# An S4 convolution beside a gated linear unit: the second factor of the kernel K built from 33 angles instead of by doublings, on one core

## The chip, the core and the metric

The kernel runs on one core of a Trainium2 chip. The engines named below are TensorE (PE, with PEld for its weight loads), VectorE (DVE), ScalarE (ACT), GpSimd (POOL) and SyncE (SP), whose queue issues all of this kernel's transfers. Each engine runs its own instructions in order and waits on semaphores for the others. The metric is the time of one execution on the device in microseconds, the median over runs; single executions vary by about one per cent.

## What is computed

From `x` (2048 positions, 512 channels) the reference mixes two results, `g` being one sigmoid for each position:

```python
g = sigmoid((x * gate_w).sum(-1))
# a: diagonal state space model, 128 complex states for each channel
logdA = dt * A;  dB = dt * Bc                      # dt = exp(log_dt)
K = einsum("dn,dnl,dn->dl", Cc, exp(logdA[:, :, None] * l), dB).real   # l = 0 .. 2047
y = irfft(rfft(pad(u)) * rfft(pad(K))) + u * Dskip # long convolution of length 2048
# b: gated linear unit
h = sigmoid(x @ w_gate) * (x @ w_up)               # 512 -> 1792
b = h @ w_down                                     # 1792 -> 512
out = g * a + (1 - g) * b
```

Everything is fp32. The part that matters here is `K`: for each of 512 channels and 2048 positions a sum over 128 states of a coefficient times a power of a complex number.

## The kernel before

The work has two threads. One is the convolution: `rows` (16 blocks of `x`: the gate's sums, a first transform, written to DRAM), `kgen` (the kernel `K`, 16 groups of 32 channels, its first transform, written to DRAM), `finish` (16 steps over frequencies: second transforms of `u` and `K`, their product, an inverse transform) and `final` (16 blocks: last transform, mixing, output). The other is `glu`, a generator which issues the gated linear unit in pieces. `UNITS` = 2016 counts its matmuls of 512 columns: 1344 in `hidden` (L401, three for each product, since every fp32 operand is split in a high and a low part) and 672 in the down projection (L339). `run_b(n)` draws pieces until n more units are dealt out.

The program deals these units out between the steps of the convolution: 24 at first, `ROW` = 32 after every fourth block of `rows`, `MID` = 50 for every half group of `kgen`, then 0.7 of what is left over the 16 steps of `finish`, and the rest in `final`. The order in the program gives the instructions their priority; a scheduler of the framework then puts each engine's instructions into a fixed order, so pieces of `glu` and `kgen` are mixed on every engine.

`kgen` has the 128 states in the partitions and for each channel d needs K at 2048 = 32 x 64 positions. A position is split in two numbers, and the power into two factors; `kps` (L220) sums over the states with one matmul for each channel and for the real and the imaginary part, [32 x 64] at a time. Before, both factors are built by doublings on DVE. `bases(pp, gi)` (L147) loads the group's parameters and gives `bz`, the 11 powers z^(2^k) of the step exp(dt A): 704 angles and exponents (L162), rounded (L163, L164), one Exp, Abs and two Sin of 352 elements on ACT (L165 to L168), and the product (L171). `double` (L180) extends a row of powers to twice its length by a complex product: three DVE instructions, L187 to L189. The tile `T` holds three parts: the first factor with the coefficient, and the two halves of the second factor. Four of the doublings (L207 to L209) extend both factors at once, the last of them 2048 elements for each instruction; a sixth one (L213), also 2048, makes the second half of the second factor. `bz` has two buffers, `T` one. Between the two `yield`s stand `bases` of the next group and the last doubling; behind it, at high priority, `kps`, its copy `kst` on ACT (L223), `Dskip` added on DVE (L225), 32 matmuls with `wk` (L232) and four copies `kev` on ACT (L236).

In `hidden` ACT makes `sg`, the sigmoid of a gate block (L408), DVE the product `h` (L409), ACT its high part `hh` (L410), DVE the low part `hl` (L411). `weights` splits weights in the same way (L381, L382 on ACT; L384, L385 on DVE in the first half). `rows` has two more sigmoids for each block (L361, L362). A change between Exp, Sin and Sigmoid on ACT shows in the trace as an ACT_TABLE_LOAD.

Of the kernel before, what the change touches and what calls it, by code (L numbers as in the profile page):

```python
# [28 lines left out]
P = 128  # L30
# [5 lines left out]
KS = [6, 0, 7, 1, 8, 2, 9, 3, 10, 4, 5]  # L36
NB = len(KS)
# [6 lines left out]
ROW, MID, END, LAST = 32, 50, 0.7, 0.14  # L44


def constants():
# [18 lines left out]
    for k in range(32):  # L66
# [7 lines left out]
    e2 = 2.0 ** np.array(KS)  # L74
# [3 lines left out]
        "c_pw": f(np.stack([e2, e2 / (2 * np.pi) * np.where(np.array(KS) < 6, -1, 1)]), 1, 2 * NB),  # L78
# [4 lines left out]
def body(ctx, tc, xp, xt, prm, ldt, dsk, gw, wgu, wdn, c_wu, c_wf, c_wk, c_w2, c_wv, c_pw, out):  # L83
# [22 lines left out]
    pw = cst.tile([P, 2, NB], F32, name="pw")  # L106
# [37 lines left out]
    def tmp(pp):  # L144
        return pp.tile([P, 2048], F32, tag="tmp", bufs=2, name="tmp")

    def bases(pp, gi):  # L147

        pg = pp.tile([P, 6, 32], F32, name="pg")
# [5 lines left out]
        nc.vector.tensor_tensor(aa, pg[:, 0:2], dg, op=OP.mult)  # L155
        sh = [P, 2, NB, 32]
        t = tmp(pp)
        m = NB * 32
        th, sc = (t[:, 2 * m * a:2 * m * (a + 1)].rearrange("p (c k b) -> p c k b", c=2, k=NB) for a in range(2))
        af = t[:, 4 * m:5 * m].rearrange("p (k b) -> p k b", k=NB)  # L160
        n = af.bitcast(I32)
        nc.vector.tensor_tensor(th, aa[:, :, None, :].to_broadcast(sh), pw[:, :, :, None].to_broadcast(sh), op=OP.mult)  # L162
        nc.scalar.activation(n, th[:, 1], AF.Copy)  # L163
        nc.vector.tensor_tensor(th[:, 1], th[:, 1], n, op=OP.subtract)  # L164
        nc.scalar.activation(th[:, 0], th[:, 0], AF.Exp)  # L165
        nc.scalar.activation(af, th[:, 1], AF.Abs)
        nc.scalar.activation(sc[:, 1], th[:, 1], AF.Sin, scale=2 * math.pi)
        nc.scalar.activation(sc[:, 0], af, AF.Sin, scale=-2 * math.pi, bias=hpi)  # L168

        bz = pp.tile([P, 3, NB, 32], F32, name="bz", bufs=2)  # L170
        nc.vector.tensor_tensor(bz[:, 0:2], sc, th[:, 0:1].to_broadcast(sh), op=OP.mult)  # L171
        nc.scalar.activation(bz[:, 2], bz[:, 1], AF.Copy, scale=-1.0)
        w = pp.tile([P, 3, 2, 32], F32, name="w")
        cb = lambda c: pg[:, 4 + c:5 + c].to_broadcast([P, 2, 32])
        nc.vector.tensor_tensor(w[:, 2], pg[:, 2:4], dg, op=OP.mult)
        nc.vector.tensor_tensor(w[:, 0], w[:, 2], cb(0), op=OP.mult)
        nc.vector.tensor_tensor(w[:, 1], w[:, 2], cb(1), op=OP.mult)
        return bz, w

    def double(pp, dst, src, bz, k, nd, e):  # L180
# [324 lines left out]
```

## Time and profile before

| what | value |
|---|---|
| median of three runs | 755.97 us (750.52 to 758.19) |
| the profiled execution, its own time | 753.36 us |
| its span in the trace | 751.6 us |
| busy PE, DVE, ACT | 706.8, 604.9, 375.5 us |
| granted TensorE clock, mean | 0.975 |
| bytes moved | 118.64 MB, mean 158 GB/s |

The three stages follow each other in time: `rows` and the first groups to some 104 us, `kgen` to some 565 us, then `finish` and `final`; `glu` runs beside all of them. A row of a busy time merges overlapping instructions; a mean duration is that of one instruction. A matmul of 512 columns lasts 402 ns in the trace, but the next one starts before it ends, so distances between starts tell more of TensorE than durations. In a row of groups the part behind the second bar is the idle time of the engine just before these instructions and what ended most of it.

### The profile page before, as it was taken

The numbers are of one execution on the slowest core, as the hardware profiler recorded it, in microseconds if no ns is written. First come the engines' busy times: TensorE is split into PE (matmuls) and PEld (weight loads), VectorE is DVE, ScalarE is ACT, GpSimd is POOL, SyncE is SP. The second block draws the span as 40 slices with busy tenths as digits, with TensorE's granted clock in tenths as the row PEclk, the third lists the DMA queues.
The fourth block names the chain that finished last, engine by engine and source line by source line (L and its number), as shares of the span: only waits on it lengthen the run. The fifth ranks groups of instructions, "written<-read, shape, count | busy, mean of one in ns | idle before, by whom it ended". The sixth has DMA issues, their size and how long they took to land.

```text
span 751.6 us, 12658 instructions
## 1 busy us (share of the span) xinstructions
PE 706.8 (94%) x5024; PEld 475.2 (63%) x5024; DVE 604.9 (80%) x835; ACT 375.5 (50%) x611; POOL 3.7 (0%) x36
## 2 busy tenths in 40 slices
PE   4988889998999999999999999999999999999995
PEld 3445348877888778877787787887883323333651
DVE  5888989999999999899999898999944544454343
ACT  5364645763638274655565654546134555555200
POOL 0000000000000000000000000000000000000000
PEclk9789879999999999999999999999999999999999
DMA  6768662433025033565013350531158877774587
GB/s 221 213 204 229 170 178 97 156 104 148 32 88 183 22 115 130 194 237 175 26 57 126 100 189 8 168 115 56 57 187 284 258 241 243 225 223 147 174 285 254
DMA packets 61019, 118.64 MB, mean 158 GB/s; under 512 B 8224, under 2 KB 22944, under 8 KB 59936
## 3 DMA queue, kind: packets, MB, share of 16 engines
q1 hardware_dynamic: 60960, 117.84, 48.3%
q8 instruction: 39, 0.64, 0.3%
q14 instruction: 20, 0.16, 0.1%
HBM read 75.35 MB, written 42.47 MB: 157 GB/s over the span
## 4 chain that ended last, share of the span: by engine, by line
PE 53%; DVE 28%; ACT 8%; DMA 7%; issue 3%; SPq 0%; DVEq 0%; ACTq 0%
PE gups L401 19%; PE dps L339 12%; PE fps L248 9%; DVE T L189 6%; DVE T L188 6%; DVE tmp L187 6%; PE ips L281 4%; PE fps L367 3%; DVE h L409 2%; PE kps L220 2%; DVE hl L411 2%; DMA xs<-xt 2%; PE fps L232 2%; DMA wst<-wgu 1%; PE fps L293 1%
## 5 line engine op out<-in xcount | busy, mean ns | idle before, releaser
L401 PE MATMUL gups<-xh,gu 128*128 128x512 f32 x896 | 293.9, 402 | 15.2 <-ACT gu L381 12.5
L401 PEld LDWEIGHTS gups<-xh,gu 128*128 128x128 f32 x896 | 170.0, 191 | 71.4 <-issue 16.2
L401 PE MATMUL gups<-xl,gu 128*128 128x512 f32 x448 | 179.2, 400 | 0.0
L339 PE MATMUL dps<-dnw,hh 128*128 128x512 f32 x448 | 150.2, 402 | 3.6 <-ACT hh L410 3.0
L187 DVE TENSOR_TENSOR tmp<-T,bz 128x64 f32<-128x64 f32 (+2 forms) x96 | 114.8, 1195 | 2.3 <-issue 0.2
L189 DVE TENSOR_TENSOR T<-T,tmp 128x64 f32<-128x64 f32 (+2 forms) x96 | 114.6, 1194 | 0.7
L188 DVE TENSOR_TENSOR T<-T,bz 128x64 f32<-128x64 f32 (+2 forms) x96 | 114.6, 1193 | 0.0
L339 PEld LDWEIGHTS dps<-dnw,hh 128*128 128x128 f32 x448 | 83.5, 189 | 37.5 <-issue 11.6
L401 PEld LDWEIGHTS gups<-xl,gu 128*128 128x128 f32 x448 | 85.6, 191 | 27.4 <-issue 10.3
L339 PE MATMUL dps<-dnw,hl 128*128 128x512 f32 x224 | 89.6, 401 | 3.0 <-DVE hl L411 1.7
L408 ACT ACTIVATE sg<-gups 128x512 f32<-128x512 f32 x56 | 33.5, 598 | 70.3 <-PE gups L401 69.6
L268 DVE TENSOR_TENSOR t<-fps,uf 128x512 f32<-128x512 f32 x32 | 22.0, 688 | 57.6 <-PE fps L248 47.6
L410 ACT ACTIVATE hh<-h 128x512 fp32r<-128x512 f32 x56 | 35.1, 628 | 47.9 <-DVE h L409 47.9
L409 DVE TENSOR_TENSOR h<-gups,sg 128x512 f32<-128x512 f32 x56 | 38.1, 684 | 20.4 <-PE gups L401 20.1
L339 PEld LDWEIGHTS dps<-dnw,hl 128*128 128x128 f32 x224 | 42.3, 189 | 16.5 <-DVE hl L411 3.7
L411 DVE TENSOR_TENSOR hl<-h,hh 128x512 fp32r<-128x512 f32 x56 | 38.3, 686 | 8.9 <-ACT hh L410 8.4
L381 ACT ACTIVATE gu<-wst 128x1024 fp32r<-128x1024 f32 x28 | 29.6, 1057 | 29.4 <-PE gups L401 13.8
L345 DVE SCALAR_TENSOR_TENSOR acc<-dps,omg,acc 128x512 f32<-128x512 f32 x48 | 35.5, 746 | 10.3 <-PE dps L339 10.3
L248 PE MATMUL fps<-au,w_in 128*64 128x512 f32 x128 | 42.3, 611 | 0.3 <-DVE t L268 0.3
L236 ACT ACTIVATE kev<-fps 128x256 f32<-128x256 f32 x64 | 33.8, 678 | 16.3 <-PE fps L232 15.4
L248 PE MATMUL fps<-ak,w_in 128*64 128x512 f32 x128 | 41.2, 609 | 0.0
L367 PE MATMUL fps<-u,wu 64*128 64x512 f32 x64 | 32.4, 780 | 6.6 <-DMA u<-xp 2.9
(78 smaller groups left out, 664.5 us busy)
## 6 DMA issues: line engine op xcount, KB each, us to landing
wst<-wgu SPq DMA_DIRECT2D x28, 512.0 KB, 4.5
a_u<-evu SPq DMA_DIRECT2D x32, 256.0 KB, 3.3
a_k<-kev SPq DMA_DIRECT2D x8, 1024.0 KB, 6.0
au<-a_u SPq DMA_DIRECT2D x16, 512.0 KB, 4.8
ak<-a_k SPq DMA_DIRECT2D x16, 512.0 KB, 4.2
b_s<-evb SPq DMA_DIRECT2D x32, 256.0 KB, 2.5
b_in<-b_s SPq DMA_DIRECT2D x16, 512.0 KB, 4.6
wsd<-wdn SPq DMA_DIRECT2D x28, 256.0 KB, 3.5
```

What stands on the lines that cost most here:

```text
L187: nc.vector.tensor_tensor(t2, src, sb, op=OP.mult)
L188: nc.vector.tensor_tensor(dst, src, br, op=OP.mult)
L189: nc.vector.tensor_tensor(dst, dst, t2[:, :, ::-1], op=OP.add)
L236: nc.scalar.activation(kv[i][:, s:s + 4], p4[:, :, :, 16 * i:16 * i + 16], AF.Copy)
L248: mm(p[64 * kb:64 * kb + 64], w[:, kb, 64 * c:64 * c + 64], a(kb), start=True, stop=True, tile_position=(0, 64 * kb), skip_group_check=True)
L339: mm(p, a[:, hs], dnw[:, b], start=(n == 0), stop=(n == last))
L345: nc.vector.scalar_tensor_tensor(accs[t], p, omg[:, t:t + 1], accs[t], op0=OP.mult, op1=OP.add)
L367: mm(ph[jp], wu[r, jp], u[r], start=True, stop=True, tile_position=(64 * jp, 0))
L401: mm(p, gu[:, a, k, dc], b[:, dc], start=(n == 0), stop=(n == 11))
L409: nc.vector.tensor_tensor(h, pp[1], sg, op=OP.mult)
L410: nc.scalar.activation(hh, h, AF.Copy)
L411: nc.vector.tensor_tensor(hl, h, hh.bitcast(F32), op=OP.subtract)
```

## The change

The second factor is no longer built by doublings. Its entry q, for q = 0 to 63, is the magnitude exp(q Re) times the cosine and sine of q - 32 angles; the rotation by 32 angles that this leaves out goes into the first factor's coefficient. Since the cosine of -k is that of k and the sine its negative, 33 angles (0 to 32) serve for all 64 entries. `bases` now computes for each of 32 channels 38 angles (these 33, and 64, 128, 256, 512 and 1024 for the doublings of the first factor): 1216 elements for each of product, rounding, subtraction, Abs and two Sin. Before it, the angle of one step is divided by 2 pi and rounded by itself (`tn`). The five exponentials for the doublings are one Exp of 160 elements; the 64 magnitudes of each channel are one Exp of 64 elements with that channel's exponent as a pointer scale, 32 instructions for each group, into `mg`. `B`, the second factor, is three DVE products: cosines and sines for q of 32 and more (2048 elements), and cosines, then negated sines for q under 32, read backwards (1024 each). The first factor keeps five doublings, now alone (`T` without the other halves: 64, 128, 256, 512, 1024 elements), and its coefficient is made and multiplied by that rotation in six small instructions. `ex`, `mg`, `bz` and `B` have one buffer each. `MID` goes from 50 to 45. The constants `c_pw` grow from 22 to 107 numbers. The program's scratch space for software-made DMA descriptors is set to 1024 bytes, which leaves more SBUF; the memsets on POOL and the copy L204 go.

```diff
-KS = [6, 0, 7, 1, 8, 2, 9, 3, 10, 4, 5]
-NB = len(KS)
+ANGLES = list(range(33)) + [64 << k for k in range(5)]
+NA = len(ANGLES)
...
-ROW, MID, END, LAST = 32, 50, 0.7, 0.14
+ROW, MID, END, LAST = 32, 45, 0.7, 0.14
...
     def bases(pp, gi):
...
+        tn = pp.tile([P, 32], I32, name="tn")
+        e5 = pp.tile([P, 5, 32], F32, name="e5")
+        ex = pp.tile([P, 32, 2, NA], F32, name="ex")
+        mg = pp.tile([P, 32, 64], F32, name="mg")
+        f, cs = ex[:, :, 1], ex[:, :, 0]
+        af = mg.rearrange("p d q -> p (d q)")[:, :32 * NA].rearrange("p (d a) -> p d a", d=32)
         n = af.bitcast(I32)
...
+        V.tensor_scalar(aa[:, 1], aa[:, 1], 1 / (2 * math.pi), None, op0=OP.mult)
+        A.activation(tn, aa[:, 1], AF.Copy)
+        V.tensor_tensor(aa[:, 1], aa[:, 1], tn, op=OP.subtract)
+        V.tensor_tensor(f, aa[:, 1, :, None].to_broadcast([P, 32, NA]), pw[:, None, :NA].to_broadcast([P, 32, NA]), op=OP.mult)
+        sh = [P, 5, 32]
+        V.tensor_tensor(e5, aa[:, 0:1].to_broadcast(sh), pw[:, NA:NA + 5, None].to_broadcast(sh), op=OP.mult)
+        A.activation(n, f, AF.Copy)
+        V.tensor_tensor(f, f, n, op=OP.subtract)
+        A.activation(af, f, AF.Abs)
+        A.activation(cs, af, AF.Sin, scale=-2 * math.pi, bias=hpi)
+        A.activation(f, f, AF.Sin, scale=-2 * math.pi)
+        A.activation(e5, e5, AF.Exp)
+        for d in range(32):
+            A.activation(mg[:, d], pw[:, NA + 5:], AF.Exp, scale=aa[:, 0, d:d + 1])
+        bz = pp.tile([P, 3, 5, 32], F32, name="bz")
+        trig = ex[:, :, :, 33:].rearrange("p d c k -> p c k d")
+        V.tensor_tensor(bz[:, 0::2], trig, e5[:, None].to_broadcast([P, 2, 5, 32]), op=OP.mult)
+        A.activation(bz[:, 1], bz[:, 2], AF.Copy, scale=-1.0)
...
     def kgen(pp):
...
-            for k in range(1, 5):
-                e = 2 ** k
-                double(pp, T2[:, :, :, e:2 * e], T2[:, :, :, 0:e], bz, 2 * k, 64, e)
+            T = pp.tile([P, 32, 2, 32], F32, name="T")
+            B = pp.tile([P, 32, 2, 64], F32, name="B")
+            V.tensor_tensor(w[:, 2, 0], w[:, 0, 0], w[:, 1, 1], op=OP.subtract)
+            V.tensor_tensor(w[:, 2, 1], w[:, 0, 1], w[:, 1, 0], op=OP.add)
+            V.tensor_tensor(w[:, 0], w[:, 2], ex[:, None, :, 0, 32].to_broadcast([P, 2, 32]), op=OP.mult)
+            V.tensor_tensor(w[:, 1], w[:, 2], ex[:, None, :, 1, 32].to_broadcast([P, 2, 32]), op=OP.mult)
+            V.tensor_tensor(T[:, :, 0, 0], w[:, 0, 0], w[:, 1, 1], op=OP.add)
+            V.tensor_tensor(T[:, :, 1, 0], w[:, 0, 1], w[:, 1, 0], op=OP.subtract)
+            V.tensor_tensor(B[:, :, :, 32:], ex[:, :, :, :32], mg[:, :, None, 32:].to_broadcast([P, 32, 2, 32]), op=OP.mult)
+            lo = ex[:, :, :, 32:0:-1]
+            V.tensor_tensor(B[:, :, 0, :32], mg[:, :, :32], lo[:, :, 0], op=OP.mult)
+            V.scalar_tensor_tensor(B[:, :, 1, :32], mg[:, :, :32], -1.0, lo[:, :, 1], op0=OP.mult, op1=OP.mult)
+            for k in range(4):
+                double(pp, T[:, :, :, 1 << k:2 << k], T[:, :, :, 0:1 << k], bz[:, :, k], 32, 1 << k)
             yield 1
             if gi + 1 < NG:
                 nxt = bases(pp, gi + 1)
-            double(pp, T[:, 2], T[:, 1], bz, 10, 32, 32)
+            double(pp, T[:, :, :, 16:], T[:, :, :, :16], bz[:, :, 4], 32, 16)
...
-                        mm(p[32 * j:32 * j + 32, s].rearrange("p (a b) -> p a b", a=2), T[:, 0, ch, c], T[:, 1:3, ch, c],
+                        mm(p[32 * j:32 * j + 32, s], T[:, ch, c], B[:, ch, c],
...
-    nc.sync.dma_start(pw, c_pw.to_broadcast([P, 2 * NB]).rearrange("p (a b) -> p a b", a=2))
+    nc.sync.dma_start(pw, c_pw.to_broadcast([P, NA + 69]))
...
-    nc = bacc.Bacc("TRN2", target_bir_lowering=False, num_devices=1)
+    nc = bacc.Bacc("TRN2", target_bir_lowering=False, num_devices=1, dynamic_dma_scratch_size=1024)
```

More of the change, by code (lines that the diff above doesn't have):

```diff
@@ L163, in bases @@
[L163 to L171, printed above, removed]
@@ L172, in bases @@
-        nc.scalar.activation(bz[:, 2], bz[:, 1], AF.Copy, scale=-1.0)
+        tn = pp.tile([P, 32], I32, name="tn")
[4 more added lines that the diff above has]
+        af = mg.rearrange("p d q -> p (d q)")[:, :32 * NA].rearrange("p (d a) -> p d a", d=32)
+        n = af.bitcast(I32)
+        V.tensor_tensor(aa, pg[:, 0:2], dg, op=OP.mult)
+        V.tensor_scalar(aa[:, 1], aa[:, 1], 1 / (2 * math.pi), None, op0=OP.mult)
```

39 lines of the change are left out of this document (11 added, 28 removed).

## The prediction

> **What bounds the kernel now.** I read the page first (busy times, then the chain that ended last), then cut the span into three stages with the windows view, at the ACT copies of the second and the sixteenth group's `kps` (L223, at 103.73 and 548.15 us), and then took prices of single instructions.
>
> ```profile
> PE 706.8 (94%) x5024; PEld 475.2 (63%) x5024; DVE 604.9 (80%) x835; ACT 375.5 (50%) x611; POOL 3.7 (0%) x36
> ...
> PE 53%; DVE 28%; ACT 8%; DMA 7%; issue 3%; SPq 0%; DVEq 0%; ACTq 0%
> PE gups L401 19%; PE dps L339 12%; PE fps L248 9%; DVE T L189 6%; DVE T L188 6%; DVE tmp L187 6%; PE ips L281 4%; PE fps L367 3%; DVE h L409 2%; PE kps L220 2%; DVE hl L411 2%; DMA xs<-xt 2%; PE fps L232 2%; DMA wst<-wgu 1%; PE fps L293 1%
> ```
>
> TensorE is busy 94% and half of the chain, but DVE holds 28% of the chain, most of it the doublings L187 to L189. The windows tell where (columns: stretch, length, busy us and instructions of PE, PEld, DVE, ACT, POOL, then granted clock, DMA share, GB/s):
>
> ```profile
> 0.00:103.73 103.73, 80.59 (x462) 44.99 (x462) 85.95 (x153) 51.04 (x101) 0.63 (x8) 0.84 0.70 205
> 103.73:548.15 444.42, 432.25 (x3879) 348.87 (x3880) 428.08 (x543) 244.63 (x377) 3.03 (x28) 1.00 0.34 114
> 548.15:751.60 203.45, 193.91 (x686) 81.31 (x686) 90.84 (x140) 79.85 (x133) 0.00 (x0) 0.99 0.70 230
> ```
>
> Stage A (rows and the first two groups) is 103.7 us, stage B (14 groups of `kgen`) 444.4, stage C (`finish`, `final`) 203.5. In B, DVE is busy 428.1 of 444.4 (96%), 30.6 us per group; ACT only 244.6 (55%), 17.5 per group. A group takes 31.7 us.
>
> PE's busy time overstates it, since matmuls overlap. What PE must issue is worked out from runs without a gap: 18 GLU matmuls in 4.08 us, 0.227 us for each unit; and a group's 128 `kps` and 32 `wk` matmuls take 1.97 (`wk`, L232) and 1.99 us (`kps`, L220). The chain by time (start, length) and the timeline have the rows:
>
> ```profile
> 412.56 4.08 PE dps L339 x18
> ...
> 736.07 4.04 DMA out<-o
> 742.12 4.59 DMA b_in<-b_s
> ```
>
> ```profile
> 402.64 1.97 PE L232 MATMUL fps<-wk,kst 128*64 128x128 f32 x32
> ...
> 427.26 1.99 PE L220 MATMUL kps<-T 128*32 128x64 f32 x128
> ```
>
> The GLU matmuls that ran in B (windows by line: L401, then L339; the count stands behind PE's busy time):
>
> ```profile
> 103.73:548.15 444.42, 257.75 (x1087) 202.25 (x1088) 1.00 0.34 114
> ...
> 103.73:548.15 444.42, 128.27 (x516) 94.66 (x516) 1.00 0.34 114
> ```
>
> 1603 units in 14 groups are 114.5 a group: 26.0 us, and with `kps` and `wk` 30.0 of 31.7. So in B, DVE is full and PE waits for it only 1.8 us per group, 25 us in all. This is what a lighter DVE can win there; the rest of PE's work is the same before and after. In C, PE is busy 193.9 of 203.5, and nothing of the change is in C but the units moved there.
>
> **The change, part by part.** DVE's prices:
>
> ```profile
> L187 DVE TENSOR_TENSOR tmp<-T,bz 128x2048 f32<-128x2048 f32 x32 | 73.1, 2285 | 0.2
> ...
> L187 DVE TENSOR_TENSOR tmp<-T,bz 128x1024 f32<-128x1024 f32 x16 | 19.5, 1221 | 0.3
> ...
> L171 DVE TENSOR_TENSOR bz<-tmp 128x704 f32<-128x704 f32 x16 | 14.2, 885 | 0.1
> L162 DVE TENSOR_TENSOR tmp<-aa,pw 128x704 f32<-128x704 f32 x16 | 14.1, 883 | 0.0
> ...
> L187 DVE TENSOR_TENSOR tmp<-T,bz 128x64 f32<-128x64 f32 x16 | 4.3, 269 | 1.1
> ...
> L177 DVE TENSOR_TENSOR w<-w,pg 128x64 f32<-128x64 f32 x16 | 3.5, 219 | 0.0
> ```
>
> From 1024 and 2048 elements a product costs 0.157 us and 1.04 ns per element. Removed per group: doublings 3 x (0.27 + 0.42 + 0.69 + 1.22 + 2 x 2.29) = 21.5; the bases' three large products 0.88 + 0.89 + 0.52, four of 0.22 and two of 0.21: 3.6. Together 25.1. Added: two products of 32 x 38 = 1216 elements, 1.42 each; two of 160 and 320, 0.32 and 0.49; twelve small ones of `aa`, `w` and `T` at 0.21, 2.5; `B` from 2048 elements and twice 1024, 2.29 + 2 x 1.22 = 4.7; five doublings of one factor alone 3 x (0.27 + 0.29 + 0.42 + 0.69 + 1.22) = 8.7. Together 19.5. DVE saves 5.6 us per group, 30.6 to 25.0. `B` reads 32 angles backwards, which no row shows; the nearest rows, 1024 and 2048 elements, bound such an op at 1.22 and 2.29, so at worst 2 us of the 5.6 are lost, and DVE is still under PE. I take 1.22.
>
> ACT's prices and table loads:
>
> ```profile
> L381 ACT ACTIVATE gu<-wst 128x1024 fp32r<-128x1024 f32 x28 | 29.6, 1057 | 29.4 <-PE gups L401 13.8 <-DMA wst<-wgu 13.5 <-issue 2.0
> L408 ACT ACT_TABLE_LOAD x22 | 28.2, 1283 | 0.7 <-PE gups L401 0.4
> L167 ACT ACT_TABLE_LOAD x16 | 20.5, 1283 | 0.3
> L165 ACT ACT_TABLE_LOAD x15 | 19.2, 1283 | 0.2
> ...
> L343 ACT ACTIVATE acc<-dps,omg 128x512 f32<-128x512 f32 x16 | 10.8, 684 | 15.8 <-PE dps L339 15.6
> ...
> L368 ACT ACTIVATE evu<-fps 128x512 f32<-128x512 f32 x16 | 9.5, 591 | 15.0 <-PE fps L367 14.2 <-DMA a_u<-evu 0.6
> L168 ACT ACTIVATE tmp<-tmp,hpi 128x352 f32<-128x352 f32 x16 | 9.2, 577 | 0.0
> L167 ACT ACTIVATE tmp<-tmp 128x352 f32<-128x352 f32 x16 | 8.0, 499 | 0.2
> ...
> L204 ACT ACTIVATE T<-bz 128x64 f32<-128x64 f32 x16 | 5.0, 315 | 0.0
> ```
>
> 352 and 1024 elements give 0.21 us and 0.83 ns per element, and a pointer operand adds 0.08 to 0.09 (L168 against L167, L343 against L368). Back to back, each starts 0.09 us before the one ahead ends:
>
> ```profile
> 73.64 0.20 ACT L361 ACTIVATE g<-gl 128x1 f32<-128x1 f32 x1
> 73.73 0.19 ACT L362 ACTIVATE omg<-gl 128x1 f32<-128x1 f32 x1
> 73.82 0.19 ACT L361 ACTIVATE g<-gl 128x1 f32<-128x1 f32 x1
> ```
>
> Removed per group: six of 352 elements and L204, 7 instructions, 3.4 us less 7 x 0.09 = 2.7. Added: three of 1216 elements at 1.22 and one with a pointer at 1.30, `tn`, `e5` and the negated copy 0.24 + 2 x 0.34, and 32 exponentials of 64 elements with a pointer scale. The last are shown by no row: below by the one-element sigmoids (0.09 from start to start), above by L204's 0.315 plus the pointer's 0.09 less the overlap, 0.31. I take the line, 0.207 + 0.053 + 0.082 - 0.09 = 0.25, nearest to L204 in size but without its scattered output: 8.0 us. Added in all 3 x 1.13 + 1.21 + 0.65 + 8.0 = 13.2, net 10.5 us per group (5.4 to 12.4 between the ends).
>
> Then the table loads. Each change of function set costs 1.28 us, and a sigmoid that falls between two sines brings two:
>
> ```profile
> 163.97 1.28 ACT L167 ACT_TABLE_LOAD   x1
> 165.26 0.50 ACT L167 ACTIVATE tmp<-tmp 128x352 f32<-128x352 f32 x1
> 165.78 1.28 ACT L408 ACT_TABLE_LOAD   x1
> 167.07 0.60 ACT L408 ACTIVATE sg<-gups 128x512 f32<-128x512 f32 x1
> 167.56 0.62 ACT L382 ACTIVATE dnw<-wsd 128x512 fp32r<-128x512 f32 x1
> 168.21 1.28 ACT L168 ACT_TABLE_LOAD   x1
> 169.50 0.59 ACT L168 ACTIVATE tmp<-tmp,hpi 128x352 f32<-128x352 f32 x1
> ```
>
> Loads before are 22 + 16 + 15 and a few more, 3.7 per group, three of them unavoidable. In B 1087 / 24 = 45 sigmoids `sg` fall (24 matmuls for each), 3.2 a group. The exponentials take some 8 us of ACT alone, 10 to 11 with what is put between; 1.0 `sg` should fall among them, two loads, in place of 0.1 now: I take 1.8 extra loads, 2.3 us, with 0 and 4 (5.1 us) as ends. Fewer GLU units per group (below) take off 10 x 0.08 = 0.8 (per 100 units 2.8 x 1.2 of `sg` and `hh`, 1.4 x 1.7 of weights, 2 of the rest). ACT: 17.5 + 10.5 + 2.3 - 0.8 = 29.5 us per group. It takes DVE's place as the fullest engine. The exponentials are short and wait for little, so I let it be busy 98% where DVE reached 96%: 30.1 us per group.
>
> The Trainium skill (ScalarE: Activation LUTs, What ACT_TABLE_LOAD costs) puts a switch at about 2.66 us, a 1.28 us load and a 1.38 us drain. In the rows above the next activation starts 0.01 us behind the load and the load 0.02 us behind the one before: the trace shows no drain. By the page's price the 1.8 extra loads would cost 4.8 us per group and the sum would be 35 us longer, 786.
>
> A new ring: `ex` and `mg` have one buffer, so `f` of the next group is written when `B` has been built. `f` 1.4, round 1.2, subtract 1.4, abs 1.2, load 1.3, two sines 2.5, load 1.3, `e5` 0.3, exponentials 8.0, `B` 4.7: 23.3 us, under a group's 30; it binds only with ACT's other work in it, which the 30.1 holds. The matmuls of `kps` keep their number and shape. The two memsets on POOL were off the path. `pw` is 107 floats a partition instead of 22, one transfer on SP's queue in the same place, hidden by the loads of the start. Queues and other DMAs stay.
>
> Units: 90 instead of 100 are dealt out per group, 140 fewer in B, 1463 or 104.5 a group if as many are taken besides as now (203). PE needs 23.7 + 4.0 = 27.7, and waits 2.4 us per group instead of 1.8.
>
> The sum against the profiled execution's 751.6:
> - A: two groups save 11 us of DVE (86 of 103.7 busy) and bring some 25 us to ACT (51 busy): gain 4, from 0 to 11.
> - B: 14 x 30.1 = 421.4, gain 23.
> - C: 140 units x 0.227 = 31.8 longer, less what fills PE's gaps. The end waits for transfers (the rows at 736 and 742 us above) and can't be filled; I take 7, from 0 to 20: cost 25.
>
> 751.6 - 4 - 23 + 25 = 749.6, and 1.8 outside the span (753.36 against 751.6): 751 us, 0.7% under the median 755.97 and 0.3% under the profiled execution. The expected gain of DVE goes to ACT.
>
> **The rivals.**
> - *ACT has room and PE is fed (faster).* For it: ACT is at 55% in B, and DVE's 5.6 us leave for certain. If the extra loads don't come, ACT needs 27.2 and PE's 27.7 bind; PE's waits in B fall from 25 us to some 10, A gives 8 and C's filling 7: 751.6 - 30 + 1.8 = 723 at best; with half an extra load per group, waits of 13 us and A as above, 751.6 - 12 - 4 - 7 + 1.8 = 730. It decides where ACT is under 27.7. Against it: sigmoids already cut the sines apart.
> - *ACT's table loads make it the bound (slower).* If each `sg` and each pause in the sines lets exponentials slip in, 3.6 extra loads come: ACT 31.8, at 98% 32.5 per group, 14 x 32.5 = 455; 751.6 - 4 + 11 + 25 + 1.8 = 785. It decides from some 30.5 on, at two and a half loads. For it: three loads within 6 us in the rows above. Against: over the whole run they are 3.7 a group. An exponential at 0.31 would add 1.9 and weigh nearly as much.
> - *A load also drains the engine.* If every extra load cost as much again as its 1.28, 2.3 us per group would come on top: ACT 31.8, as in the slower rival, 785. The rows above speak against it. This is the skill's rule (ScalarE: Activation LUTs).
>
> **How the numbers follow.** About 1% (748 to 764 around the median) is what can be told from no change. Forecast 0.42, its own range 740 to 766 (B's period 0.9 us either way, A's and C's bounds); faster rival 0.33; slower rival 0.23; draining loads 0.02. Faster by over 1%: 0.31 of the faster rival and 0.09 of the forecast's low end, 0.40. Slower: 0.22, 0.02 and 0.08 of its high end, 0.32. Within 1%: 0.28. The range is 722, the faster rival at its best, to 788, just over the slower one's time; the tenths left out are a still slower exponential and a faster A.
>
> **What would show it.** Right: in B, DVE busy falls from 96% to about 83% and ACT rises from 55% to over 95%; the exponentials' group reads about 0.34 us and 7 to 8 us per group; table loads rise from 59 to 85 to 95; groups 30 us apart; C about 25 us longer. Wrong: ACT under 90% with PE's waits gone (faster rival), over 110 loads with groups 32 us or more apart (slower rival), or exponentials far from 0.34 us.

## The result, and the profile after

The change makes the kernel slower: 836.22 us (median of four runs, 834.15 to 837.46) against 753.63 us for the kernel before on the same chip; the ratio is 1.109, with a 95% interval of 1.102 to 1.116. The prediction said 751 us, and its range ended at 788. The profiled execution of the changed kernel took 834.15 us, 832.4 of them in the span.

The page of the changed kernel, busy times and then the chain that ended last:

```profile
PE 730.7 (88%) x5024; PEld 484.5 (58%) x5024; DVE 517.1 (62%) x947; ACT 583.6 (70%) x1165; POOL 0.2 (0%) x4
...
PE 41%; ACT 36%; DVE 15%; DMA 5%; issue 3%; SPq 0%; DVEq 0%; ACTq 0%
PE gups L414 13%; PE dps L352 10%; ACT mg L176 10%; PE fps L261 9%; PE ips L294 4%; ACT L176 3%; ACT kev L249 3%; ACT L421 2%; DVE B L217 2%; ACT L172 2%; ACT ex L172 2%; ACT ex L173 2%; ACT mg L171 2%; DMA out<-o 2%; ACT sg L421 2%
```

DVE's work fell from 604.9 to 517.1 us, ACT's rose from 375.5 to 583.6, and ACT took DVE's place in the chain (36% instead of 8%), with the 32 exponentials of each group (L176) at its head. But no engine is full. The windows of the three stages, cut at the same two copies `kst` (columns as in the prediction):

```profile
0.00:122.36 122.36, 81.39 (x474) 44.40 (x476) 78.78 (x173) 96.45 (x197) 0.20 (x4) 0.79 0.62 182
122.36:588.63 466.27, 417.03 (x3711) 329.71 (x3708) 339.09 (x621) 398.23 (x823) 0.00 (x0) 0.96 0.30 102
588.63:832.40 243.77, 232.24 (x844) 110.41 (x844) 99.18 (x153) 88.95 (x147) 0.00 (x0) 0.97 0.62 201
```

All three stages grew: A from 103.7 to 122.4, B from 444.4 to 466.3 and C from 203.5 to 243.8 us. TensorE has 5024 matmuls before and after. Of the 80.8 us by which the span grew, it is idle for 56.9 (17.9 in A, 37.0 in B, 2.0 in C) and busy longer for 23.9. In B a group takes 33.3 us. DVE is busy 24.2 us of it (73%) and ACT 28.4 (85%). TensorE's groups of stage B show what it gets in that time (busy, mean ns, then idle time ahead and what ended it):

```profile
L414 PE MATMUL gups<-xh,gu 128*128 128x512 f32 x643 | 212.6, 404 | 13.2 <-ACT sg L421 9.2 <-ACT gu L394 3.3 <-DVE gu L397 0.6
L414 PE MATMUL gups<-xl,gu 128*128 128x512 f32 x322 | 129.6, 403 | 0.0
L352 PE MATMUL dps<-dnw,hh 128*128 128x512 f32 x320 | 110.9, 408 | 15.1 <-ACT hh L423 13.1 <-issue 1.3 <-ACT acc L356 0.7
L352 PE MATMUL dps<-dnw,hl 128*128 128x512 f32 x160 | 64.9, 408 | 6.2 <-DVE hl L424 6.1
```

These are 1445 units, 103.2 per group: 23.4 us at 0.227, 27.4 with `kps` and `wk`. So PE loses 5.9 us per group, where it lost 1.8 before. Not all of that is idle time: PE is idle for 49.2 us of B, 3.5 per group, against 12.2 us before, and B's mean granted clock is 0.96 instead of 1.00, which is worth up to another 19 us. Some 26 of the 49 idle us end with ACT: with `sg`, `hh`, the weights' copy `gu` and `acc`. The same view of the kernel before has 1.6 us for `sg` and 1.2 for `hh`:

```profile
L401 PE MATMUL gups<-xh,gu 128*128 128x512 f32 x725 | 229.7, 392 | 2.4 <-ACT sg L408 1.6 <-ACT xh L310 0.8
...
L339 PE MATMUL dps<-dnw,hh 128*128 128x512 f32 x344 | 112.3, 395 | 1.8 <-ACT hh L410 1.2 <-DVE acc L345 0.4
```

ACT's own groups in stage B:

```profile
L176 ACT ACTIVATE mg<-pw,aa 128x64 f32<-128x64 f32 x435 | 111.3, 337 | 0.4
L176 ACT ACT_TABLE_LOAD x31 | 39.8, 1283 | 11.7 <-DVE aa L160 11.3
L421 ACT ACT_TABLE_LOAD x29 | 37.2, 1283 | 2.0 <-PE gups L414 1.5
...
L423 ACT ACTIVATE hh<-h 128x512 fp32r<-128x512 f32 x40 | 24.5, 622 | 16.4 <-DVE h L422 16.4
...
L395 ACT ACTIVATE dnw<-wsd 128x512 fp32r<-128x512 f32 x20 | 12.5, 624 | 10.0 <-PE dps L352 7.0 <-DMA wsd<-wdn 3.1
```

ACT is idle 68 us of B, and the last column tells why: it stands at `hh` until DVE has `h` (16.4 us), at a table load for the next group's exponentials until DVE has `aa` (11.3), at a weight copy until PE frees its buffer (7.0). These are waits in the middle of an in-order queue: what stands behind them waits too. The wait view of B (who waited for whom: us in all, times, longest) has the other side: the largest wait of all is that of DVE, for the exponentials.

```profile
DVE B L217 <- ACT mg L176: 49.1, 12, 6.5
PEld dps L352 <- ACT hh L423: 18.6, 13, 3.0
```

What stands behind the exponentials in ACT's queue waits as well. Here `h` was ready at 377.17, its copy `hh` came behind 19 exponentials at 388.15, and PE stood idle until it had it (timeline: start, length, instruction, then the idle time before it):

```profile
376.49 0.68 DVE L422 TENSOR_TENSOR h<-gups,sg 128x512 f32<-128x512 f32 x1
...
383.36 4.65 ACT L176 ACTIVATE mg<-pw,aa 128x64 f32<-128x64 f32 x19
...
388.15 0.61 ACT L423 ACTIVATE hh<-h 128x512 fp32r<-128x512 f32 x1
...
388.81 0.94 PE L352 MATMUL dps<-dnw,hh 128*128 128x512 f32 x2 [2.59 <-ACT hh L423]
```

Over the 40 `hh` of B, the copy starts on average 4.7 us after its `h` is ready, against 0.3 us before the change; of these 188 us ACT spends 112 on the exponentials.

How one group hangs together is read from the chain by time (start, length, what), from one rounding of angles to the next:

```profile
401.29 1.28 ACT L421
402.57 0.01 issue
402.58 0.60 ACT sg L421
403.18 1.12 ACT mg L168
...
404.32 1.44 DVE ex L169
...
405.78 1.22 ACT mg L171
...
408.32 1.33 ACT ex L172
...
412.89 0.97 ACT kev L249 x2
...
414.21 0.99 ACT kev L249 x2
...
416.64 2.26 ACT mg L176 x9
...
418.92 2.29 DVE B L217
...
425.45 0.15 DVE aa L160
...
427.66 2.87 ACT mg L176 x12
430.53 0.48 ACT hh L423
...
431.48 1.21 ACT mg L168
```

The rounding `mg` (L168) of one group starts at 403.18, that of the next at 431.48, and nearly every step between them is ACT or waits for ACT; `sg`, two pairs of `kev` and `hh` are served in the same queue in between. One thing I had not seen in the code: the rounding needs only the first 32 x 38 = 1216 elements of `mg`, the room of channels 0 to 18. The exponentials of the other 13 channels may run ahead of it, and here 1 + 12 of them do. They bring a second change of table in the group: L176 has 40 loads in 16 groups.

### The profile page after: what moved, and what is told of

It is laid out like the page before. It is cut to its first block, busy times and chain, and to the rows that moved or that the text cites. A ratio compares the mean times of both kernels' runs of the same rounds, so it can differ in the third digit from the quotient of the medians.

```text
span 832.4 us, 13211 instructions
## 1 busy us (share of the span) xinstructions
PE 730.7 (88%) x5024; PEld 484.5 (58%) x5024; DVE 517.1 (62%) x947; ACT 583.6 (70%) x1165; POOL 0.2 (0%) x4
## 4 chain that ended last, share of the span: by engine, by line
PE 41%; ACT 36%; DVE 15%; DMA 5%; issue 3%; SPq 0%; DVEq 0%; ACTq 0%
PE gups L414 13%; PE dps L352 10%; ACT mg L176 10%; PE fps L261 9%; PE ips L294 4%; ACT L176 3%; ACT kev L249 3%; ACT L421 2%; DVE B L217 2%; ACT L172 2%; ACT ex L172 2%; ACT ex L173 2%; ACT mg L171 2%; DMA out<-o 2%; ACT sg L421 2%
## 5 line engine op out<-in xcount | busy, mean ns | idle before, releaser
L414 PE MATMUL gups<-xh,gu 128*128 128x512 f32 x896 | 298.6, 406 | 33.0 <-ACT gu L394 23.1
L414 PEld LDWEIGHTS gups<-xh,gu 128*128 128x128 f32 x896 | 171.4, 193 | 93.1 <-ACT gu L394 25.2
L414 PE MATMUL gups<-xl,gu 128*128 128x512 f32 x448 | 182.6, 408 | 0.0
L352 PE MATMUL dps<-dnw,hh 128*128 128x512 f32 x448 | 161.8, 421 | 18.4 <-ACT hh L423 16.5
L176 ACT ACTIVATE mg<-pw,aa 128x64 f32<-128x64 f32 x512 | 131.8, 337 | 1.6 <-DVE aa L160 1.1
L352 PE MATMUL dps<-dnw,hl 128*128 128x512 f32 x224 | 92.0, 412 | 6.2 <-DVE hl L424 6.1
L217 DVE TENSOR_TENSOR B<-ex,mg 128x2048 f32<-128x2048 f32 x16 | 36.7, 2293 | 53.8 <-ACT mg L176 53.7
L421 ACT ACTIVATE sg<-gups 128x512 f32<-128x512 f32 x56 | 32.9, 597 | 39.8 <-PE gups L414 39.4
L176 ACT ACT_TABLE_LOAD x40 | 51.3, 1283 | 13.0 <-DVE aa L160 12.5
L196 DVE TENSOR_TENSOR T<-T,bz 128x64 f32<-128x64 f32 (+4 forms) x80 | 46.1, 577 | 0.6
L197 DVE TENSOR_TENSOR T<-T,tmp 128x64 f32<-128x64 f32 (+4 forms) x80 | 46.1, 576 | 0.3
L195 DVE TENSOR_TENSOR tmp<-T,bz 128x64 f32<-128x64 f32 (+4 forms) x80 | 45.9, 573 | 0.3
L233 PE MATMUL kps<-B,T 128*32 128x64 f32 x2048 | 36.2, 234 | 10.5 <-DVE T L197 8.0
L380 PE MATMUL fps<-u,wu 64*128 64x512 f32 x64 | 30.9, 798 | 16.2 <-DMA u<-xp 13.6
```

The source lines that it names most:

```text
L176: A.activation(mg[:, d], pw[:, NA + 5:], AF.Exp, scale=aa[:, 0, d:d + 1])
L195: nc.vector.tensor_tensor(t2, src, sb, op=OP.mult)
L196: nc.vector.tensor_tensor(dst, src, br, op=OP.mult)
L197: nc.vector.tensor_tensor(dst, dst, t2[:, :, ::-1], op=OP.add)
L217: V.tensor_tensor(B[:, :, :, 32:], ex[:, :, :, :32], mg[:, :, None, 32:].to_broadcast([P, 32, 2, 32]), op=OP.mult)
L233: mm(p[32 * j:32 * j + 32, s], T[:, ch, c], B[:, ch, c], start=(c == 0), stop=(c == 1), tile_position=(0, 32 * j), skip_group_check=True)
```

## The experiments

Theory R (ring) said that the one buffer each of `ex`, `mg` and `aa` makes a group's steps follow each other and so sets its length. Theory L (load) said that the exponentials and their table loads take too much of ACT, a queue which also feeds the GLU. Then there is the plain third thing, `MID`. All runs are single executions beside one of the kernel before on the same chip (750.5 to 759.8 us). Single executions differ by about one per cent, so only larger differences count below. The table has the runs on which the argument rests; the times of the other six stand in the last of these sections. In it, A, B and C are the stages; then come group length, units (by the count of matmuls), ACT and DVE busy per group in B; "PE waits" is the length less 0.227 for each unit and 4.0, so it also holds what a lower clock costs.

| kernel | time | A | B | C | group | units | ACT | DVE | PE waits | loads |
|---|---|---|---|---|---|---|---|---|---|---|
| before | 753.4 | 103.7 | 444.4 | 203.5 | 31.7 | 114.5 | 17.5 | 30.6 | 1.8 | 59 |
| after | 834.2 | 122.4 | 466.3 | 243.8 | 33.3 | 103.2 | 28.4 | 24.2 | 5.9 | 101 |
| 1 after, MID 50 | 798.1 | 120.9 | 468.5 | 206.9 | 33.5 | 113.9 | 29.5 | 24.8 | 3.6 | 107 |
| 14 after, MID 60 | 829.8 | 121.3 | 512.2 | 194.6 | 36.6 | 127.5 | 32.5 | 25.9 | 3.6 | 132 |
| 13 before, MID 45 | 778.6 | 101.3 | 436.9 | 238.6 | 31.2 | 104.4 | 16.8 | 29.9 | 3.5 | 59 |
| 3 one Exp, MID 45 | 767.8 | 92.2 | 373.2 | 300.6 | 26.7 | 87.4 | 21.9 | 25.4 | 2.8 | 86 |
| 15 one Exp, MID 50 | 772.3 | 94.8 | 396.6 | 279.1 | 28.3 | 93.1 | 22.9 | 26.0 | 3.2 | 95 |
| 16 Exp four times, MID 50 | 797.1 | 96.0 | 491.5 | 207.8 | 35.1 | 114.6 | 31.0 | 27.8 | 5.1 | 110 |
| 4 before, 32 more Exp | 781.9 | 111.4 | 461.8 | 206.9 | 33.0 | 113.9 | 27.6 | 30.9 | 3.1 | 116 |
| 2 two `mg`, MID 45 | 824.9 | 107.5 | 460.3 | 255.3 | 32.9 | 98.7 | 30.0 | 24.1 | 6.5 | 119 |
| 10 two `mg`, MID 50 | 804.5 | 107.4 | 467.4 | 227.9 | 33.4 | 107.1 | 30.7 | 24.7 | 5.1 | 122 |
| 6 two `ex`, MID 50 | 818.4 | 105.6 | 485.9 | 225.2 | 34.7 | 107.9 | 31.5 | 24.9 | 6.2 | 130 |
| 5 Exp behind Sin, MID 50 | 827.4 | 124.1 | 494.8 | 206.7 | 35.3 | 113.9 | 26.4 | 24.8 | 5.5 | 64 |
| 9 two `ex`, Exp behind Sin, MID 50 | 803.5 | 120.1 | 454.1 | 227.5 | 32.4 | 107.1 | 27.6 | 24.4 | 4.1 | 80 |

### The number of units dealt out

Run 1 undoes it in the changed kernel, run 13 makes it alone in the kernel before, run 14 goes the other way.

```diff
-ROW, MID, END, LAST = 32, 45, 0.7, 0.14
+ROW, MID, END, LAST = 32, 50, 0.7, 0.14
```

> MID back to 50, nothing else. Theory R (a ring: the next group's angles and exponentials wait for the one buffer of ex, mg and aa that B reads, and B waits for them, so a group takes 33 us while ACT is only 85% busy): B keeps its 33.3 us per group, 155 units leave C, 834 falls to about 800. Theory L (ACT is simply too full: its queue with 32 exponentials and some 100 table loads sets the group): more units per group bring ACT work, B grows by 10 to 15 us, C gives 35, about 812. If MID were what made it slow, back to about 755.

> The kernel before with 45 units dealt out per half group instead of 50, nothing else. If the units taken out of the 14 groups are worth their matmul time there (0.227 us each, about 140 of them: 32 us), stage B falls from 444 to about 415 and the time stays near 752. If the groups are held by the work that makes K (DVE 30.6 us per group before), B stays between 430 and 444, C grows from 203 to 235 to 243, and the time is 775 to 790: then the lower number costs in the kernel before just what it costs after.

> The changed kernel with 60 units dealt out per half group instead of 45. If the groups of about 33.4 us are held by the chain that makes K (ring and exponentials) and PE has slack in them, the units fill it: B grows little (470 to 490), C falls to 170 to 185, time 765 to 785. If the units' own ScalarE and TensorE work is what makes a group long, as theory L (ScalarE too full) has it, each unit dealt out adds its 0.227 us or more: B 500 to 530, and the time stays at 795 to 815.

B and C of run 1 in the windows view:

```profile
120.91:589.38 468.47, 438.29 (x3861) 349.00 (x3858) 347.44 (x633) 413.19 (x841) 0.00 (x0) 0.99 0.31 105
589.38:796.30 206.92, 196.34 (x694) 82.48 (x694) 91.21 (x141) 80.99 (x135) 0.00 (x0) 0.98 0.70 229
```

B and C of run 13:

```profile
101.31:538.21 436.90, 406.66 (x3737) 328.20 (x3738) 418.98 (x528) 234.85 (x362) 3.04 (x28) 0.97 0.32 107
538.21:776.80 238.59, 226.73 (x828) 107.07 (x828) 100.04 (x154) 90.06 (x148) 0.00 (x0) 0.99 0.66 212
```

B and C of run 14:

```profile
121.29:633.47 512.18, 481.14 (x4039) 384.85 (x4036) 363.18 (x651) 454.62 (x879) 0.00 (x0) 0.98 0.29 98
633.47:828.10 194.63, 161.17 (x504) 50.64 (x504) 79.06 (x123) 73.11 (x122) 0.00 (x0) 0.90 0.73 237
```

With 50 units the changed kernel gains 38 us (836.2 to 798.1), all of it in C: B is as long with 1595 units as with 1445. The ten units fewer per group, 34 us of matmuls, became idle time of PE (49.2 us of B instead of 30.2) and a slower clock (0.96 instead of 0.99). In the kernel before the same edit costs 28 us (750.5 to 778.6): C grows by 35.1, B gives 7.5 back and then stands at DVE's 29.9 us per group, 96% busy. So 45 for 50 is a loss of 28 to 38 us by itself. The other way does not pay either: 60 units lengthen B by 43.7 us for 190 units, 0.230 each, which is just their matmul time, and C falls by only 12.3, since `finish` and `final` have too little PE work left to fill it (161.2 busy of 194.6). I read this so: at 50, PE's time and the chain of K are about level; above it PE sets the group, below it the chain.

### The exponentials' time on ACT

Runs 3 and 15 replace the 32 small exponentials by one DVE product and one Exp of 2048 elements (with 45 and with 50 units).

```diff
-        for d in range(32):
-            A.activation(mg[:, d], pw[:, NA + 5:], AF.Exp, scale=aa[:, 0, d:d + 1])
+        V.tensor_tensor(mg, aa[:, 0, :, None].to_broadcast([P, 32, 64]), pw[:, None, NA + 5:].to_broadcast([P, 32, 64]), op=OP.mult)
+        A.activation(mg, mg, AF.Exp)
```

Run 16 takes run 15 and runs this Exp four times, three of them into a tile `mj` that nobody reads. Run 4 adds 32 exponentials of zeros, into such a tile too, to the kernel before (whose scratch space is 1024 bytes there, to make room):

```diff
+        mj = pp.tile([P, 32, 64], F32, name="mj")
+        for d in range(32):
+            nc.scalar.activation(mj[:, d], z64, AF.Exp, scale=aa[:, 0, d:d + 1])
```

> The 32 exponentials of a group become one DVE product of 2048 elements (2.3 us) and one Exp of 2048 (1.9 us instead of 8.0). Both theories expect a gain: R because the ring loses 4 us (8.0 - 1.9 - 2.3), a group of about 29 us, 775; L because ACT loses 6 us a group and up to 25 table loads, a group of about 27 us, 745. Loads should fall from 101 to under 75.

> The kernel before, with 32 exponentials of 64 zeros per group into a tile that nobody reads (8 us of ACT per group added, the output is the reference's). Theory L: ACT goes from 55% to over 80% in B with as many table loads as after, 800 or more. Theory R: the load alone, with nothing waiting for it, costs little, 755 to 775.

> The changed kernel with 50 units, and the 32 exponentials replaced by one product on DVE (2.3 us) and one exponential of 2048 elements (about 1.9 us). Beside the same kernel with 32 exponentials (798): ScalarE loses about 6 us per group, DVE gains 2.3 and is the fuller one. Expected B 380 to 400, 27 to 28.5 us per group, time 765 to 780. It is the partner of the run with four such exponentials.

> As the run before, but the exponential of 2048 elements is run four times, three of them into a tile that nobody reads: about 7.6 us of ScalarE per group, as the 32 small ones take, in 4 instructions with one wait. If it is the exponentials' time on ScalarE that holds the group (in front of hh, sg and the weights' copies), the time goes back to 790 to 805 and the group to about 32 to 33 us. If it is the small pieces (their starts, and table loads between them), it stays within 15 us of the run with one exponential.

A and B of run 3:

```profile
0.00:92.19 92.19, 63.49 (x418) 36.47 (x420) 78.25 (x166) 68.87 (x100) 0.20 (x4) 0.83 0.60 184
92.19:465.41 373.22, 354.97 (x3520) 282.17 (x3521) 355.26 (x623) 307.20 (x390) 0.00 (x0) 0.98 0.39 126
```

B of run 4:

```profile
111.41:573.25 461.84, 436.19 (x3875) 348.94 (x3876) 432.30 (x548) 387.09 (x844) 2.83 (x26) 0.99 0.34 111
```

B and C of run 15:

```profile
94.78:491.37 396.59, 372.99 (x3599) 297.12 (x3600) 363.89 (x631) 320.50 (x404) 0.00 (x0) 0.98 0.36 118
491.37:770.50 279.13, 267.63 (x1010) 140.78 (x1010) 109.64 (x167) 98.96 (x161) 0.00 (x0) 0.98 0.60 196
```

B of run 16:

```profile
95.99:587.52 491.53, 459.26 (x3905) 358.20 (x3904) 388.61 (x666) 434.67 (x497) 0.00 (x0) 0.96 0.35 113
```

At 45 units one Exp takes 68 us off (836.2 to 767.8), though ACT was only 85% busy. ACT's work falls by 6.5 us per group and the group by 6.6, but this is not a rate of one to one: B also has 15.8 units fewer per group, which are 3.6 us of matmuls and go to C. DVE then is the full engine (95%). At 50 units the gain is 26 us (798.1 to 772.3). Run 16 gives these 25 us back (797.1) with about the same time on ACT in 4 instructions instead of 32.

The stages alone mislead here, since units move between them. Taken together, A and B are 589.4 us with 1739 units in run 1, 491.4 with 1423 in run 15 and 587.5 with 1729 in run 16. From run 1 to run 15, 316 units at 0.227 are 72 of the 98 us; the other 26 are the gain. Run 16 stands where run 1 stands. So for the whole time it is the exponentials' time on ACT and not their being small pieces. For the parts this is not shown: run 16 has the short A of one Exp (96.0), and its groups (35.1) are longer than those of run 1 (33.5).

In runs 15 and 16 the exponentials stand in the ring as well. Run 4 has no ring of `ex` and `mg`: in a kernel with nothing else of the change they cost 31 us, with a reader for none of the results, while DVE keeps its 30.9 us. At most the next group's `aa` waits until they have read it; what else they delay is work on ACT. Its 781.9 lies between what the two theories had said. The number of loads rises there too (59 to 116), and `hh` starts only 0.7 us after its `h`; how the 31 us divide between exponentials and loads was not taken apart.

With one Exp, the two settings of `MID` no longer differ by more than the noise (767.8 and 772.3): the 38 us above hold only while the exponentials hold the group.

### The ring and the table loads

Runs 2 and 10 give `mg`, `aa`, `w` and the small tiles a second buffer, run 6 `ex` and the small tiles; no run gives two buffers to both `mg` and `ex`. Run 5 lets the exponentials be issued only behind the second sine, so that none runs early, and run 9 has both edits of runs 6 and 5.

```diff
-        mg = pp.tile([P, 32, 64], F32, name="mg")
+        mg = pp.tile([P, 32, 64], F32, name="mg", bufs=2)
```

```diff
-        A.activation(f, f, AF.Sin, scale=-2 * math.pi)
-        A.activation(e5, e5, AF.Exp)
-        for d in range(32):
-            A.activation(mg[:, d], pw[:, NA + 5:], AF.Exp, scale=aa[:, 0, d:d + 1])
+        sn = A.activation(f, f, AF.Sin, scale=-2 * math.pi)
+        with tc.issue_after(getattr(sn, "ins", sn)):
+            A.activation(e5, e5, AF.Exp)
+            for d in range(32):
+                A.activation(mg[:, d], pw[:, NA + 5:], AF.Exp, scale=aa[:, 0, d:d + 1])
```

> Two buffers for mg and for the small tiles aa, tn, e5, pg, dt, w; same work. Theory R: the exponentials no longer wait for B of the group before, a group falls from 33.3 to about 29 to 30 us (ACT 28.4 busy), 770 to 790. Theory L: the same ACT work in the same queue, within 10 us of 834.

> MID 50, two buffers for ex and for aa, tn, e5, pg, dt: the next group's angles, sines and rounding no longer wait for B. The program has 130 table loads instead of 107 (30 us of ACT more). Theory R: the ring is broken on its longest part, a group falls below 31 us, 765 or less. Theory L: more loads, 800 to 820.

> MID 50 and two buffers for mg, aa, tn, e5, pg, dt, w, no order (122 table loads). With MID 45 this gave A 107 us instead of 122 and B 32.9 us per group. A again near 107; B 33 to 34 by the loads; about 785 to 790, 10 under MID 50 alone.

> MID 50, and e5 and the 32 exponentials stand behind the group's second sine in ACT's order, none of them early; same instructions, but 64 table loads stand in the program instead of 107 (55 us of ACT less). Theory L with the table loads as the heavy part: B falls by about 2.5 us per group, 798 to about 760. Theory R: the 12 or so exponentials that ran early now stand in the ring, 3 us per group more, 800 to 830.

> MID 50, two buffers for ex (and aa, tn, e5, pg, dt) and the exponentials behind the sines: the ring is cut and the program has 80 table loads instead of the 130 of the run with two buffers alone. Theory R with L (the ring and the loads each hold the group at 33 us, and each edit alone traded one for the other: two buffers 34.7 us with 130 loads, order 35.4 us with 64 loads and the ring): both gone, a group of 29 to 31 us, A near 105, about 750 to 765. If neither is the cause and the 8 us blocks of exponentials in ACT's queue are, the same 800 to 820.

A second buffer shortens stage A by 13 to 15 us (120.9 to 107.4 and 105.6), so the start pays for the ring; but run 9, with two `ex` and no early exponentials, has 120.1. In B it gives nothing: run 10 has the group of run 1 (33.4 and 33.5) with fewer units in it, run 6 is 1.2 us longer. In these two runs `hh` starts only 1.0 and 0.9 us after its `h` and ACT is 91 to 92% busy, so `hh` behind the exponentials is not the only way to a long group. The whole time gains 11 us at 45 units (run 2) and nothing at 50. The freer order lets ACT slip in more changes of table, 122 and 130 loads. Fewer loads do not help by themselves either. Run 5 has 43 fewer than run 1, and its B is the longest of the runs with 50 units:

```profile
124.11:618.94 494.83, 451.35 (x3871) 358.49 (x3868) 347.50 (x630) 369.48 (x811) 0.00 (x0) 0.95 0.31 101
```

ACT is busy only 75% of it: the exponentials now lie as one block of 8 us behind the sines, and `hh` starts on average 4.0 us after its `h`. Run 9 removes both the ring through `ex` and the early exponentials, and its group is still 32.4 us; the ring through `mg`, in which the rounding and the Abs are kept too, stays in it. So neither one ring alone nor the count of loads sets B. The changed kernel without any ring was not run. Runs 2 and 6 came out as theory L had said, run 5 as theory R had said. Over the runs of the changed kernel with 50 units and the exponentials' full time, loads go from 64 to 130, and the time is 827, 804, 798, 797, 805 and 818 us in that order, with the fewest and the most loads both slow.

### With one exponential: what is left, and a better version

Run 15 is still 21.8 us above the kernel before, though its groups end at 491 us instead of 548. B is 48 us shorter, but C is 76 longer: 594 instead of 270 units are left for it, and 324 x 0.227 are 73.5 us. This is work that has only moved. What is lost is lost ahead of it: A and B gave away these 73.5 us of matmuls and are only 56.8 us shorter. PE is idle for 63.0 us of the whole span instead of 44.8, and 16.2 of these 18.2 us lie in A and B. Six runs tried the rest. Runs 7 and 18 deal out 55 and 75 units, run 17 deals 56 instead of 32 after every fourth block of `rows`; run 8 has 55 units and the Exps behind the sine; runs 11 and 12 move the product to POOL, run 12 with two buffers of `ex`.

```diff
-        V.tensor_tensor(mg, aa[:, 0, :, None].to_broadcast([P, 32, 64]), pw[:, None, NA + 5:].to_broadcast([P, 32, 64]), op=OP.mult)
+        nc.gpsimd.tensor_tensor(mg, aa[:, 0, :, None].to_broadcast([P, 32, 64]), pw[:, None, NA + 5:].to_broadcast([P, 32, 64]), op=OP.mult)
```

> One product and one Exp for the magnitudes, with MID 55 instead of 45. With MID 45 B was 26.7 us per group with DVE 95% busy, and C was 301 us long for the units left. Some 23 units per group more: B about 29.5 us per group, C about 227, 735 to 745, under the kernel before.

> As the run with one exponential, but 75 units instead of 50 dealt out per half group. 50 and 55 gave the same number of units in B (1303). If the number dealt out decides, B takes up to 500 more units, C falls from 279 to about 200 and the time is 735 to 760. If the order of the engines' queues (K at higher priority) holds the units back, B still takes some 1300 and the time is 770 to 790.

> As the run with one exponential and 50 units (772), but 56 units instead of 32 are dealt out after every fourth block of rows, so 96 more units come early. With one exponential the 16 groups end 57 us earlier than in the kernel before, but 324 more units are left for stage C (594). If those units were only dealt out too late, C falls by up to 96 x 0.227 = 22 us, the groups of the start fill up, and the time is 748 to 758. If the early groups can't take more units (weights and their copies, K at higher priority), it stays at 765 to 780.

> The same, with e5 and the Exp behind the second sine: 79 table loads instead of 95 (20 us of ACT less). With DVE the fullest engine in B the loads should matter little: within 8 us of the run without the order. If the loads themselves delay PE, 10 to 20 us faster.

> The one product for the magnitudes on POOL instead of DVE, one Exp, MID 50. DVE, 95% busy in B with the product on it, falls to about 23 us per group. If POOL's product takes under 5 us, a group of 26 to 27 us with more units in B than the 87 before, 745 to 760. If it is much longer it stands in the ring and a group goes over 30.

> The same with two buffers for ex, aa, tn, e5, pg, dt: the product and the sines leave the ring. If the ring still held the group with one Exp, 10 us faster than with one buffer; if PE or DVE does, the same within 5.

The times are 784.9 (run 7), 804.0 (18), 782.6 (17), 796.2 (8), 825.9 (11) and 834.1 us (12). None beats the kernel before. Run 8 has 16 loads fewer than run 7 and is 11 us slower. Runs 7, 15 and 18 deal out 55, 50 and 75 units, and B takes 1303 in all three, in 397 to 398 us. B and C of run 18:

```profile
92.67:491.16 398.49, 373.67 (x3599) 297.35 (x3600) 364.25 (x631) 320.88 (x403) 0.00 (x0) 0.98 0.36 118
491.16:802.20 311.04, 273.63 (x1010) 144.44 (x1010) 110.51 (x167) 99.01 (x161) 0.00 (x0) 0.95 0.53 176
```

So what is dealt out no longer decides how much of the GLU runs beside K; the 594 units stay for C, and dealt out earlier they only lie worse in it (311 instead of 279 us). Run 17 got 24 more units into A, and B took 27 fewer. What holds the units back (the four buffers of weights, their copies on ACT, or K's higher priority) was not taken apart and stays open. On POOL the product took 4.2 us (run 11) instead of 2.3 and slowed DVE (last section), and `kps` waited for `T`.

## Why the prediction was wrong

Most sizes were right. DVE needs 24.2 us per group (25.0 predicted). An exponential takes 337 ns (0.34) and all of them 8.2 us per group. ACT is busy 28.4 us per group (29.5), with 103.2 units (104.5); 101 table loads came instead of 85 to 95. The Exp of 64 elements really sits where the line for small operations put it, and a load still costs 1283 ns with no gap behind it: 402.57 and 402.58 in the chain above. Over all loads of the run the median gap is 0.02 us ahead of one and 0.01 behind it, so the rival with draining loads is out. The backward products of `B` take 1.22 us, as assumed.

- **The step that failed** is the one from ACT's work to the group: "I let it be busy 98% where DVE reached 96%: 30.1 us per group." ACT is 85% busy and the group takes 33.3 us. This is 45 of the 83 us by which the sum was short. The reason given, that the exponentials "are short and wait for little", held for them alone (0.4 us of idle time before 435 of them) and not for what stands around and behind them: the load ahead of them waits 11.3 us for `aa`, and `hh` starts 4.7 us after its `h` instead of 0.3. As I read the two chains, DVE could reach 96% since it had a long chain of its own, doubling after doubling, in which each step waits only for the one before on the same engine. The new chain of K goes from ACT to DVE and back (round, subtract, Abs, Sin, Exp, `B`), and in the same in-order queue ACT serves `sg`, `hh` and weights that PE waits for. Each of these waits stops all that is queued behind it. The experiments show that the exponentials' time counts although ACT is not full: with one Exp in place of the 32 the changed kernel gains 26 us (run 15 against run 1), and 32 idle exponentials cost the kernel before 31 us (run 4). That the two chains cross on ACT is shown for `hh` in the kernel after; it does not explain runs 6 and 10, and which wait sets a group in all of them stays open.
- **The ring** was said to be 23.3 us and to bind "only with ACT's other work in it, which the 30.1 holds". With that work it is 28.3 us in the stretch shown, which is a short group. A second buffer gives 13 to 15 us in A and nothing in B, so the ring costs at the start. That a group's time holds it was right for B as far as one ring was cut at a time, though the time itself was not.
- **Stage A** was "gain 4" and lost 18.6. By work alone ACT had room (96.5 busy of 122.4). Two buffers take some 14 of it off and one Exp takes 30 off: so there, too, the exponentials cost more than DVE's doublings had. It is not their time on ACT alone: run 16 gives that back and A stays at 96.0. The gain of 4 was picked between its bounds and not worked out.
- **Stage C** was "140 units x 0.227 = 31.8 longer, less what fills PE's gaps", 25, and cost 40.3: 158 units came, 35.9 us, and nothing was filled (PE is idle 11.5 us of C, against 9.5 before, and 11.9 in run 13). The bound of "from 0 to 20" for the filling was open only to the good side.
- **Units taken out of B.** The sum let the group be set by ACT alone and so gave PE the ten units fewer as a wait of 2.4 us. Measured are 5.9, a lower clock included. In this the direction was right, but I did not draw the conclusion that moving units to C then is a pure loss: run 1 shows it, 38 us.
- **The slower rival** ended nearest (785), but not by its mechanism. It asked for extra loads that make ACT full, "groups 32 us or more apart" with "over 110 loads". Groups did come 33 us apart, with 101 loads and ACT not full, and the number of loads does not order the runs. ACT under 90% was a sign of the faster rival, but "with PE's waits gone"; they tripled. No rival had an ACT that is not full and still holds the group.

In short: of the 85.7 us between 750.5 (the kernel before, beside run 15) and 836.2, the edits undone in turn put 38 on `MID` while the exponentials stand (run 1), 26 on the exponentials' time on ACT (run 15 against run 1), and 22 remain in a kernel with neither (run 15), nearly all of it idle time of PE in A and B. The first two depend on the order: with one Exp, `MID` costs nothing that the noise would show.

## What to carry to other kernels

Work moved from a full engine to a half-empty one is not hidden by the empty half if that engine stands in the middle of other engines' chains: ask who waits behind the new block in its in-order queue, and do not count on such an engine being filled to 95% (here ACT was 75 to 92% busy in B in the runs with the exponentials' full time). Many small instructions with a pointer scalar can be one large one with a product ahead of it: 32 exponentials in 8.2 us became a product of 2.3 us on DVE and an Exp of 1.9 us. Finishing a side chain earlier is worth nothing if the main engine's work stays the same and is only moved behind it: count the main engine's waits, not the side chain's length.

## What the hardware showed that I had not expected

**Short waits were followed by half of TensorE's clock.** The mean granted clock of B fell from 1.00 to 0.96: 37.5 us of it ran at half clock, in ten stretches, where B of the kernel before had none. Four windows of the changed kernel (PE, PEld, DVE, ACT, POOL, then the granted clock):

```profile
385.00:388.40 3.40, 1.22 (x6) 0.68 (x4) 0.35 (x1) 3.40 (x15) 0.00 (x0) 1.00 0.04 14
388.40:392.60 4.20, 2.81 (x7) 1.79 (x8) 4.20 (x4) 4.17 (x7) 0.00 (x0) 0.59 0.00 0
392.60:396.00 3.40, 3.40 (x9) 2.64 (x8) 3.40 (x13) 2.32 (x3) 0.00 (x0) 0.50 0.44 154
396.00:399.40 3.40, 3.40 (x16) 2.80 (x15) 3.40 (x8) 3.39 (x15) 0.00 (x0) 1.00 0.34 106
```

From 386.2 to 388.8 PE waited 2.59 us for `hh` while ACT was busy throughout; from 389.2 to 396.0 it then ran at half clock, 9 matmuls in 3.4 us instead of 16. These 6.8 us at half clock cost some 3.4 us more, so this wait for ACT was paid more than twice. Nine of the ten stretches begin during an idle time of PE of 1.8 to 4.3 us or within 2.5 us of its end. One of 2.54 us (at 585.7) was not followed by any, so how long a wait must be is not settled here. The Trainium skill (TensorE: Matmul & The Clock Gate, HAM oscillation) describes such a throttle, with gaps of more than about 3.4 us as its rule; the shorter one here did it too.

**A DVE product stood still while POOL worked.** In run 11 (timeline: start, length, instruction), while POOL made its product, a DVE product of 512 elements that started 0.2 us later lasted 4.03 us; the one after it, without POOL, took 0.68:

```profile
318.68 3.68 POOL L175 TENSOR_TENSOR mg<-aa,pw 128x2048 f32<-128x2048 f32 x1 [26.58 <-ACT ex L172]
...
318.87 4.03 DVE L196 TENSOR_TENSOR T<-T,bz 128x512 f32<-128x512 f32 x1
...
323.01 0.68 DVE L197 TENSOR_TENSOR T<-T,tmp 128x512 f32<-128x512 f32 x1
```

The Trainium skill (SBUF — State Buffer, Who interferes with whom) says that a DVE instruction with two inputs in SBUF contends with a POOL instruction that reads SBUF; these rows agree. In 15 of run 11's 16 POOL products, a DVE instruction that ran beside it lasted between 3.1 and 4.7 us.
